# Sliding-window attention and a SoLU MLP: head pairs in one score tile, casting loads, and a list-scheduled order

## The chip, the core and the metric

The kernel runs on one core of a Trainium2 chip. TensorE (PE) multiplies matrices, VectorE (DVE) and ScalarE (ACT) do elementwise work, GpSimd (POOL) does small work and can issue transfers, SyncE (SP) issues transfers; sixteen DMA engines carry them. TensorE writes only to PSUM, 16 KB in each of 128 partitions, in eight banks of 512 fp32 columns; the other tiles lie in SBUF. The metric is the device time of one execution in microseconds (us).

## The reference

There are 4 batches of 8 heads, 768 positions and 64 dimensions per head. A query attends to the 96 latest keys (itself among them) and to the first 8 keys of the sequence, with a bias that falls with distance. The result goes through an MLP with a SoLU activation and a LayerNorm, on 3,072 tokens of 512 features with 1,024 hidden ones.

```python
scores = q @ k.T / sqrt(64)
is_global = pos_k < 8;  is_local = (0 <= rel) & (rel < 96)       # rel = pos_q - pos_k
dist = where(is_global & ~is_local, 96, abs(rel))
scores = where(is_global | is_local, scores - slope[h] * dist, -1e9)
attn = softmax(scores) @ v
x = attn.transpose(0, 2, 1, 3).reshape(3072, 512)
h = x @ w_in
solu = h * softmax(h)
ln = (solu - mean(solu)) / sqrt(var(solu) + 1e-6) * g_ln
out = ln @ w_out
```

## The kernel before

The work is written as two loops one after the other, in a framework that places semaphores and keeps each engine's instructions in program order.

First come constants: `bmask` holds, for each head, the exponential of the bias for a block of 128 keys against 256 queries, zero outside the window; `gmask` serves the global keys. The weights are loaded in fp32 by two transfers on SP (L108, L111) and cast to fp16 on VectorE (L109, L115).

The attention loop (L128) runs over batches and groups of four heads. Two heads are loaded side by side into `qq32` and `kk32` in fp32 (SP, L137 and L141), cast by ScalarE (L147, L149), transposed by TensorE in 128-column blocks into `pqQ` and `pqK` (L157, L159) and copied out by VectorE (L164, L165). v is loaded by SP (L179) and cast by POOL into `vo65`, which has a column of ones behind the 64 dimensions (L185). The global scores of four heads share the tile `psg` (L196, L201, ScalarE L207). Each head then has: six score matmuls, 128 keys against 256 queries each, into `psb` (L230); one exponential over 1,536 columns (L238); one multiplication by the mask (L249); 17 matmuls into `psav`, with the probabilities as weights and v as the moving operand, so that rows are queries and the 65th column is the divisor (L263); the reciprocal and the scaling on VectorE (L279, L285); six transposes into `pxt` (L291) and a copy into `xT` (L295), which holds the attention output with features on partitions. `psb` and `psg` share one buffer of the tag `sc`, so that a head's scores wait until the exponential of the head before has read them. `xT` holds all 3,072 tokens.

The MLP loop (L309) runs over 24 tiles of 128 tokens: eight matmuls into `ph` (L313), the exponential with its sum (L322), `solu` (L328), the mean, the sum of squares `sq` (L336), the centred `smc` (L342), eight transposes `lT` (L348), a copy `lTs` (ScalarE, L352), eight matmuls into `po` (L355) and a copy into `ouall` (L359). Only after all 24 tiles are the variances turned into `rstdall` (L361 to L378), with a square root on ScalarE that needs another function table, and each tile is then scaled and stored (L382, L386).

Of the kernel before, what the change touches and what calls it, by code (L numbers as in the profile page):

```python
# [9 lines left out]
FP32 = mybir.dt.float32  # L10
FP16 = mybir.dt.float16
I32 = mybir.dt.int32
AF = mybir.ActivationFunctionType
ALU = mybir.AluOpType

P = 128


@with_exitstack
def kernel(  # L20
# [12 lines left out]
    nc = tc.nc  # L33
# [5 lines left out]
    NSB = S // P  # L39
    NQB = 2 * P  # L40
# [3 lines left out]
    LNSC = 1024.0  # L44
# [4 lines left out]
    const = ctx.enter_context(tc.tile_pool(name="const", bufs=1))  # L49
    big = ctx.enter_context(tc.tile_pool(name="big", bufs=1))  # L50

    ident = const.tile([P, P], FP16, name="ident")
    nc.gpsimd.memset(ident, 0.0)
    nc.gpsimd.affine_select(
        out=ident, in_=ident, compare_op=ALU.not_equal, fill=1.0,
        base=0, pattern=[[-1, P]], channel_multiplier=1,
    )

    diff_i = const.tile([P, NQB], I32, name="diff_i")
    nc.gpsimd.iota(diff_i, pattern=[[1, NQB]], base=0, channel_multiplier=-1)  # L60
    diff_f = const.tile([P, NQB], FP32, name="diff_f")
    nc.vector.tensor_copy(diff_f, diff_i)
    nc.vector.tensor_scalar_max(out=diff_f, in0=diff_f, scalar1=0.0)
    bmask = const.tile([P, H, NQB], FP16, name="bmask")
    for h in range(H):
        nc.scalar.activation(out=bmask[:, h, :], in_=diff_f, func=AF.Exp,
                             scale=-slopes[h])
    bm_flat = bmask.rearrange("p h f -> p (h f)")
    nc.gpsimd.affine_select(
        out=bm_flat, in_=bm_flat, compare_op=ALU.is_ge, fill=0.0,  # L70
        base=0, pattern=[[0, H], [1, NQB]], channel_multiplier=-1,
    )
    nc.gpsimd.affine_select(
        out=bm_flat, in_=bm_flat, compare_op=ALU.is_ge, fill=0.0,
        base=NL - 1, pattern=[[0, H], [-1, NQB]], channel_multiplier=1,
    )

    gmask = const.tile([P, P], FP16, name="gmask")
    glow = const.tile([P, P], FP16, name="glow")
    nc.gpsimd.memset(glow, 1.0)  # L80
    nc.gpsimd.affine_select(
        out=glow, in_=glow, compare_op=ALU.is_gt, fill=0.0,
        base=0, pattern=[[-1, P]], channel_multiplier=1,
    )
    nc.gpsimd.memset(gmask, 1.0)
    nc.gpsimd.affine_select(
        out=gmask, in_=gmask, compare_op=ALU.is_ge, fill=0.0,
        base=-NL, pattern=[[1, P]], channel_multiplier=-1,
    )
    nc.vector.tensor_add(gmask, gmask, glow)  # L90
    gmaskq = const.tile([P, P], FP16, name="gmaskq")
    nc.gpsimd.memset(gmaskq, 1.0)
    for g in range(4):
        nc.vector.tensor_copy(gmaskq[32 * g : 32 * g + NG], gmask[0:NG])

    gbias4 = const.tile([P, 2], FP32, name="gbias4")
    for gi in range(2):
        for g in range(4):
            nc.vector.memset(
                gbias4[32 * g : 32 * (g + 1), gi : gi + 1],  # L100
                -float(NL) * slopes[4 * gi + g],
            )

    w_in_sb = const.tile([P, NCC, D_FF], FP16, name="w_in_sb")
    gw_out_sb = const.tile([P, NFC, D_MODEL], FP16, name="gw_out_sb")
    with tc.tile_pool(name="wtmp", bufs=1) as wtmp:
        w_in32 = wtmp.tile([P, NCC, D_FF], FP32, name="w_in32")
        nc.sync.dma_start(out=w_in32, in_=moe_w_in.rearrange("(j p) f -> p j f", p=P))  # L108
        nc.vector.tensor_copy(w_in_sb, w_in32)  # L109
        w_out32 = wtmp.tile([P, NFC, D_MODEL], FP32, name="w_out32")  # L110
        nc.sync.dma_start(out=w_out32, in_=moe_w_out.rearrange("(j p) c -> p j c", p=P))  # L111
        g32 = wtmp.tile([P, NFC], FP32, name="g32")
        nc.sync.dma_start(out=g32, in_=moe_g_ln.rearrange("(j p) -> p j", p=P))
        for j in range(NFC):
            nc.vector.tensor_scalar_mul(  # L115
                out=gw_out_sb[:, j, :], in0=w_out32[:, j, :],
                scalar1=g32[:, j : j + 1],
            )

    xT = big.tile([P, NCC, N_TOK], FP16, name="xT")  # L120

    with tc.tile_pool(name="apsum", bufs=1, space=bass.MemoryType.PSUM) as apsum, \
         tc.tile_pool(name="asb", bufs=3) as asb, \
         tc.tile_pool(name="ahsb", bufs=6) as ahsb, \
         tc.tile_pool(name="ajsb", bufs=4) as ajsb, \
         tc.tile_pool(name="agsb", bufs=3) as agsb:

        for b in range(B):  # L128
            for gi in range(2):
                qTs, kTs, vo65s = [], [], []  # L130
                vg65 = agsb.tile([P, 65], FP16, name="vg65")
                for pj in range(2):
                    j0 = 4 * gi + 2 * pj
                    qq32 = asb.tile([P, NSB, 2 * D], FP32, name="qq32")
                    kk32 = asb.tile([P, NSB, 2 * D], FP32, name="kk32")
                    for m in range(2):
                        nc.sync.dma_start(  # L137
                            out=qq32[:, :, m * D : m * D + D],
                            in_=q[b, j0 + m].rearrange("(a p) d -> p a d", p=P),
                        )  # L140
                        nc.sync.dma_start(  # L141
                            out=kk32[:, :, m * D : m * D + D],
                            in_=k[b, j0 + m].rearrange("(a p) d -> p a d", p=P),
                        )
                    qq16 = asb.tile([P, NSB, 2 * D], FP16, name="qq16")
                    kk16 = asb.tile([P, NSB, 2 * D], FP16, name="kk16")
                    nc.scalar.copy(out=qq16.rearrange("p a d -> p (a d)"),  # L147
                                   in_=qq32.rearrange("p a d -> p (a d)"))
                    nc.scalar.copy(out=kk16.rearrange("p a d -> p (a d)"),  # L149
                                   in_=kk32.rearrange("p a d -> p (a d)"))  # L150

                    pqQ = apsum.tile([P, NSB, P], FP16, name="pqQ",
                                     space=bass.MemoryType.PSUM, tag="pq", bufs=2)
                    pqK = apsum.tile([P, NSB, P], FP16, name="pqK",
                                     space=bass.MemoryType.PSUM, tag="pq", bufs=2)
                    for a in range(NSB):
                        nc.tensor.transpose(out=pqQ[:, a, :],  # L157
                                            in_=qq16[:, a, :], identity=ident)
                        nc.tensor.transpose(out=pqK[:, a, :],  # L159
                                            in_=kk16[:, a, :], identity=ident)  # L160
                    qTt = ajsb.tile([P, NSB + 1, P], FP16, name="qTt")
                    kTt = ajsb.tile([P, NSB, P], FP16, name="kTt")
                    nc.gpsimd.memset(qTt[:, NSB, :], 0.0)
                    nc.vector.tensor_copy(out=qTt[:, 0:NSB, :], in_=pqQ)  # L164
                    nc.vector.tensor_copy(out=kTt, in_=pqK)  # L165
                    for m in range(2):
                        qTs.append(
                            qTt[64 * m : 64 * m + D].rearrange("d a p -> d (a p)")
                        )
                        kTs.append(  # L170
                            kTt[64 * m : 64 * m + D].rearrange(
                                "d a p -> d (a p)"
                            )
                        )

                    for m in range(2):
                        g = 2 * pj + m
                        v32 = asb.tile([P, NSB, D], FP32, name="v32")
                        nc.sync.dma_start(  # L179
                            out=v32,  # L180
                            in_=v[b, j0 + m].rearrange("(a p) d -> p a d", p=P),
                        )
                        vo65 = ahsb.tile([P, NSB, 65], FP16, name="vo65")
                        nc.gpsimd.memset(vo65[:, :, D : D + 1], 1.0)
                        nc.gpsimd.tensor_copy(out=vo65[:, :, 0:D], in_=v32)  # L185
                        vo65s.append(vo65)
                        nc.vector.tensor_copy(
                            out=vg65[32 * g : 32 * g + NG], in_=vo65[0:NG, 0, :]
                        )
# [232 lines left out]
```

## Time and profile before

| quantity | value |
|---|---|
| median of 3 runs | 334.15 us (332.35 to 337.17) |
| span of the profiled execution | 335.8 us |
| busy: PE, DVE, ACT, POOL | 247.5, 191.3, 144.8, 28.9 us |
| DMA | 29.65 MB in 81,349 packets, 76,720 of them under 512 bytes |
| DMA share of 16 engines | 38.4% |
| from issue to landing, one head of q, k, v | 3.9, 4.2, 3.8 us |

The profile is of one execution. An engine is busy while an instruction of its own runs; matmuls overlap, and their ends are modelled, so that the distance from start to start tells more of TensorE's rate than the mean duration does. A group is written as line, engine, operation, output and inputs, shapes, count, then busy time and mean time of one, then the idle time just before and what ended it. The chain of waits is followed back from the last instruction to whatever released each step.

### The profile page before, as it was taken

The numbers are of one execution on the slowest core, as the hardware profiler recorded it, in microseconds if no ns is written. First come the engines' busy times: TensorE is split into PE (matmuls) and PEld (weight loads), VectorE is DVE, ScalarE is ACT, GpSimd is POOL, SyncE is SP. The second block draws the span as 40 slices with busy tenths as digits, with TensorE's granted clock in tenths as the row PEclk, the third lists the DMA queues.
The fourth block names the chain that finished last, engine by engine and source line by source line (L and its number), as shares of the span: only waits on it lengthen the run. The fifth ranks groups of instructions, "written<-read, shape, count | busy, mean of one in ns | idle before, by whom it ended". The sixth has DMA issues, their size and how long they took to land.

```text
span 335.8 us, 4686 instructions
## 1 busy us (share of the span) xinstructions
PE 247.5 (74%) x1760; PEld 140.0 (42%) x1760; DVE 191.3 (57%) x450; ACT 144.8 (43%) x179; POOL 28.9 (9%) x94
## 2 busy tenths in 40 slices
PE   0005797996969789798897887999889898895400
PEld 0002454664646466564664533444444444442100
DVE  1523364572756656364464528685965957865653
ACT  4012652536544363651634304655565656554100
POOL 7002101121101211110100000000000000000000
PEclk9999999999995755555555559999999999997755
DMA  7679966662777665368000000000000000000586
GB/s 273 227 143 217 196 125 126 127 127 47 142 143 141 142 126 107 60 133 164 2 0 0 2 0 0 2 0 2 2 0 2 0 0 2 0 0 1 197 302 250
DMA packets 81349, 29.65 MB, mean 88 GB/s; under 512 B 76720, under 2 KB 76720, under 8 KB 81328
## 3 DMA queue, kind: packets, MB, share of 16 engines
q1 hardware_dynamic: 81328, 29.37, 38.4%
q8 instruction: 13, 0.21, 0.3%
q14 instruction: 8, 0.07, 0.1%
HBM read 23.07 MB, written 6.29 MB: 87 GB/s over the span
## 4 chain that ended last, share of the span: by engine, by line
PE 49%; ACT 18%; DVE 16%; DMA 10%; issue 4%; SPq 2%; DVEq 0%; ACTq 0%
PE psb L230 13%; PE po L355 9%; PE psav L263 8%; ACT eb L238 7%; PE pxt L291 6%; DVE solu L328 6%; DMA out_dram<-osb 4%; DMA g<-in_moe_g_ln_dram 4%; ACT lTs L352 3%; PE pqK L159 3%; PE pqQ L157 3%; PE psg L196 3%; DVE sq L336 3%; ACT e L322 3%; PE ph L313 2%
## 5 line engine op out<-in xcount | busy, mean ns | idle before, releaser
L238 ACT ACTIVATE eb<-psb 128x1536 f16<-128x1536 f32 x32 | 46.4, 1451 | 52.0 <-PE psb L230 51.7
L230 PE MATMUL psb<-qTt,kTt 64*128 64x256 f16 x192 | 45.6, 395 | 18.9 <-ACT eb L238 15.0
L313 PE MATMUL ph<-w_in_sb,xT 128*128 128x512 f16 x192 | 49.9, 394 | 7.2 <-DVE solu L328 6.6
L355 PE MATMUL po<-gw_out_sb,lTs 128*128 128x512 f16 x192 | 48.4, 398 | 5.0 <-ACT lTs L352 3.8
L249 DVE TENSOR_TENSOR eb<-eb,bmask 128x1536 f16<-128x1536 f16 x32 | 30.5, 952 | 19.3 <-ACT eb L238 19.3
L230 PEld LDWEIGHTS <-kTt 64*128 64x128 f16 x192 | 22.0, 125 | 34.8 <-issue 26.5
L157 PE MATMUL pqQ<-ident,qq 128*128 128x128 f16 x96 | 14.9, 309 | 27.1 <-ACT qq L147 27.1
L355 PEld LDWEIGHTS <-lTs 128*128 128x128 f16 x192 | 17.9, 101 | 39.0 <-ACT lTs L352 20.1
L328 DVE SCALAR_TENSOR_TENSOR solu<-e,r,ph 128x1024 f16<-128x1024 f16 x24 | 30.7, 1280 | 2.7 <-DVE r L325 0.3
L322 ACT ACTIVATE e<-ph 128x1024 f16<-128x1024 f32 x24 | 24.6, 1027 | 15.7 <-PE ph L313 15.6
L359 ACT CAST ouall<-po 128x512 f16<-128x512 f32 x24 | 14.1, 586 | 36.7 <-PE po L355 36.7
L336 DVE CUSTOM_DVE_ANT_0 sq<-solu 128x1024 f16<-128x1024 f16 x24 | 29.2, 1216 | 0.0
L291 PE MATMUL pxt<-ident,onrm 128*64 128x128 f16 x192 | 26.1, 305 | 2.2 <-DVE onrm L285 2.1
L313 PEld LDWEIGHTS <-xT 128*128 128x128 f16 x192 | 18.4, 101 | 22.1 <-issue 5.5
L352 ACT COPY lTs<-lT 128x1024 f16<-128x1024 f16 x24 | 24.3, 1011 | 7.2 <-PE lT L348 7.2
L279 DVE RECIPROCAL rl<-psav 128x6 f32<-128x6 f32 x32 | 6.3, 196 | 33.5 <-PE psav L263 33.3
L263 PE MATMUL psav<-vo,eb 128*128 128x65 f16 x352 | 25.1, 243 | 0.0
L295 DVE COPY xT<-pxt 64x768 f16<-64x768 f16 x32 | 17.6, 549 | 12.7 <-PE pxt L291 12.6
L291 PEld LDWEIGHTS <-onrm 128*64 128x64 f16 x192 | 18.7, 159 | 14.2 <-DVE onrm L285 9.3
L263 PEld LDWEIGHTS <-eb 128*128 128x128 f16 x352 | 20.9, 130 | 7.8 <-issue 4.4
L147 ACT CAST qq<-qq 128x768 f16<-128x768 f32 x16 | 13.2, 824 | 22.7 <-DMA qq<-in_q_dram 22.7
L157 PEld LDWEIGHTS <-qq 128*128 128x128 f16 x96 | 9.4, 137 | 32.4 <-ACT qq L147 29.9
(63 smaller groups left out, 253.5 us busy)
## 6 DMA issues: line engine op xcount, KB each, us to landing
qq<-in_q_dram SPq DMA_DIRECT2D x32, 192.0 KB, 3.9
kk<-in_k_dram SPq DMA_DIRECT2D x32, 192.0 KB, 4.2
v<-in_v_dram SPq DMA_DIRECT2D x32, 192.0 KB, 3.8
out_dram<-osb SPq DMA_DIRECT2D x24, 256.0 KB, 2.0
w_in<-in_moe_w_in_dram SPq DMA_DIRECT2D x1, 2048.0 KB, 7.9
w_out<-in_moe_w_out_dram SPq DMA_DIRECT2D x1, 2048.0 KB, 13.9
g<-in_moe_g_ln_dram SPq DMA_DIRECT2D x1, 4.0 KB, 13.7
```

What stands on the lines that cost most here:

```text
L157: nc.tensor.transpose(out=pqQ[:, a, :], in_=qq16[:, a, :], identity=ident)
L230: nc.tensor.matmul(out=psb[:, cj, :], lhsT=kT[:, ts(cj, P)], rhs=qTp[:, ds(P * cj, NQB)], start=st, stop=not st,)
L238: nc.scalar.activation(out=eb.rearrange("p a f -> p (a f)"), in_=psb.rearrange("p a f -> p (a f)"), func=AF.Exp, scale=inv_sqrt_d,)
L249: nc.vector.tensor_tensor(out=eb.rearrange("p a f -> p (a f)"), in0=eb.rearrange("p a f -> p (a f)"), in1=bm_ap, op=ALU.mult,)
L263: nc.tensor.matmul(out=psav[:, rb, :], lhsT=lhs, rhs=rhs_ap, start=st, stop=last, tile_position=tp,)
L291: nc.tensor.transpose(out=pxt[0:D, rb, :], in_=onrm[:, rb, :], identity=ident,)
L313: nc.tensor.matmul(out=ph[:, ds(fh * 512, 512)], lhsT=xT[:, j, ts(tb, P)], rhs=w_in_sb[:, j, ds(fh * 512, 512)], start=(j == 0), stop=(j = ...
L322: nc.scalar.activation(out=e, in_=ph, func=AF.Exp, accum_out=s0)
L328: nc.vector.scalar_tensor_tensor(out=solu, in0=e, scalar=r, in1=ph, op0=ALU.mult, op1=ALU.mult, accum_out=s1,)
L336: nc.vector.tensor_tensor_reduce(out=sq, in0=solu, in1=solu, scale=1.0, scalar=0.0, op0=ALU.mult, op1=ALU.add, accum_out=s2all[:, tb : tb ...
L352: nc.scalar.copy(out=lTs, in_=lT)
L355: nc.tensor.matmul(out=po, lhsT=lTs[:, u, :], rhs=gw_out_sb[:, u, :], start=(u == 0), stop=(u == NFC - 1),)
```

## The change

The kernel is written anew around one list of steps.

*Scores.* A block is now 56 local keys; the 8 global keys stand beside them, which makes 64 rows. Two heads share the 128 rows of one score tile: matmuls of one head use rows 0 to 63 of the array, those of the other rows 64 to 127. Each block meets the 152 queries that can see it. A row of 768 queries is cut into two score groups, of 1,008 columns each, in the single PSUM tile `sc`. `mask` holds the exponential of the bias in the same layout, global keys included.

*Outputs.* v goes into `vbd`, a tile with the two heads' values in the two diagonal quarters and zeros in the others. It is the weight, the probabilities are the moving operand, and the result stands transposed, with features on partitions, as the MLP needs it; `pxt` and its copies are gone. The divisors come from matmuls with ones (`onesd`), then Ln and Exp(-x) on ScalarE (`lns`, `rr`), and a transfer on SP that spreads each pair's two rows over 128 partitions (`rb`). Sums, divisors, value matmuls and `xT` are made per half row of 384 queries.

*Loads.* All loads of q, k, v, w_in and w_out are issued by POOL and write fp16 (w_out stays fp32); the casts are gone. The global values are loaded once (`vg16`) and copied by SP into each batch's `vbd`.

*MLP.* The mean is taken out of the weights (`weight_rows`, `weight_mean`, `weight_sub`), and `uu` is e times h, divided by no sum: the LayerNorm's scale takes it in. The squares go to ScalarE. Statistics are made for three tiles at a time, by Ln and Exp(-x/2), so that there is one function table; each tile is scaled while it is copied out of PSUM and stored at once.

*Order.* `Plan` takes every step with its engine, an assumed duration, a target time, its dependencies and the buffers that it takes and frees, and places the steps in time: on each engine, of the steps that are ready, the one with the earliest target goes first. The instructions are issued in that order. Targets interleave batch b's attention with the MLP tiles of earlier rows.

```diff
+class Plan:
+    def order(self):
...
+                while heap:
+                    tgt, i = heapq.heappop(heap)
+                    s = steps[i]
+                    if s["take"] is not None and not pools[s["take"]]:
+                        kept.append((tgt, i))
+                        continue
...
+    sc_ps = [ps.tile([P, 2, 512], FP32, name="sc")]
+    ph_ps = [ps.tile([P, D_FF], FP32, name="ph")]
+    po_ps = [ps.tile([P, D_MODEL], FP32, name="po")]
+    ta_ps = [ps.tile([P, 512], FP32, name=f"ta{i}") for i in range(3)]
...
+    def load_rows(src, dst, b, p, lo, hi):
+        for h in range(2):
+            nc.gpsimd.dma_start(
+                out=dst[:, lo:hi, h, :],
+                in_=src[b, 2 * p + h].rearrange("(a p) d -> p a d", p=P)[:, lo:hi])
...
+                nc.gpsimd.dma_start(
+                    out=dst[part : part + BLK, c0 : full[-1] + 1 : 2, p, 64 * h : 64 * h + D],
+                    in_=src)
...
+    vz_st = step("POOL", 8.0, 24.0, [], lambda: nc.gpsimd.memset(vbd[1], 0.0))
...
-                    for cj in range(NSB):
-                        nc.tensor.matmul(
-                            out=psb[:, cj, :],
-                            lhsT=kT[:, ts(cj, P)],
-                            rhs=qTp[:, ds(P * cj, NQB)],
...
+                        for c, q0, w, par, col in PIECES[gi] + PADS[gi]:
+                            for h in range(2):
+                                o = 64 * (h ^ par)
+                                nc.tensor.matmul(
+                                    out=sc[o : o + 64, par, col : col + w],
+                                    lhsT=kk[64 * h : 64 * h + D, c, :],
+                                    rhs=qq[64 * h : 64 * h + D, q0 : q0 + w],
+                                    start=True, stop=True, tile_position=(64 * h, o),
+                                )
...
+                        nc.tensor.matmul(
+                            out=sp[32 * p : 32 * p + 32, lo : lo + w], lhsT=onesd[:, par, :],
+                            rhs=eb[e_st[p, gi][0]["slot"]][:, par, col : col + w],
...
+                            tile_position=(0, 32 * p), skip_group_check=True,
...
+                    nc.sync.dma_start(
+                        out=rb[ri_["slot"]],
+                        in_=bass.AP(tensor=a.tensor, offset=a.offset,
+                                    ap=[a.ap[0], [0, 4], [1, HS]]))
...
+                        nc.tensor.matmul(
+                            out=o[:, lo : lo + w], lhsT=vbd[vi["slot"]][:, c, p, :],
+                            rhs=eb[e_st[p, gi][0]["slot"]][:, par, col : col + w],
...
-            nc.vector.scalar_tensor_tensor(
-                out=solu, in0=e, scalar=r, in1=ph,
-                op0=ALU.mult, op1=ALU.mult, accum_out=s1,
-            )
+        u["fn"] = lambda u=u, ex=ex, gidx=gidx, gcol=gcol: nc.vector.scalar_tensor_tensor(
+            out=uu[u["slot"]], in0=ef[ex["slot"]], scalar=USC, in1=ph_ps[0],
+            op0=ALU.mult, op1=ALU.mult, accum_out=s1[gidx][:, gcol : gcol + 1])
...
+                ou["fn"] = lambda ou=ou, gidx=gidx, x=x: nc.scalar.activation(
+                    out=osb[ou["slot"]], in_=po_ps[0], func=AF.Copy,
+                    scale=rstd[gidx][:, x % 3 : x % 3 + 1])
...
+    for s in plan.order():
+        if s["fn"] is not None:
+            s["fn"]()
```

## The prediction

> **What bounds the kernel now.** I read four views, in this order. The first is a table of stages: the span cut at the points where the work changes, with the busy time of each engine (instructions in brackets), the granted clock, the DMA share and GB/s.
>
> ```profile
> 0.00:32.00 32.00, 4.11 (x28) 2.36 (x28) 9.97 (x30) 7.16 (x13) 8.28 (x27) 1.00 0.86 215
> 32.00:197.00 165.00, 138.89 (x1156) 90.16 (x1156) 90.43 (x194) 73.79 (x68) 20.65 (x67) 0.72 0.52 99
> 197.00:312.00 115.00, 101.63 (x570) 46.73 (x571) 79.49 (x204) 63.25 (x97) 0.00 (x0) 0.96 0.00 1
> 312.00:335.80 23.80, 2.92 (x8) 0.76 (x6) 11.45 (x24) 0.59 (x1) 0.00 (x0) 0.57 0.71 264
> ```
>
> There are four stages one after the other: 32 us of loading weights, 165 us of attention, 115 us of MLP, 24 us in which the output is only scaled and stored. The DMA engines are empty for 115 us, TensorE nearly so for the 56 us of the outer two.
>
> The second view is the page's chain of work that ended last.
>
> ```profile
> PE 49%; ACT 18%; DVE 16%; DMA 10%; issue 4%; SPq 2%; DVEq 0%; ACTq 0%
> PE psb L230 13%; PE po L355 9%; PE psav L263 8%; ACT eb L238 7%; PE pxt L291 6%; DVE solu L328 6%; DMA out_dram<-osb 4%; DMA g<-in_moe_g_ln_dram 4%; ACT lTs L352 3%; PE pqK L159 3%; PE pqQ L157 3%; PE psg L196 3%; DVE sq L336 3%; ACT e L322 3%; PE ph L313 2%
> ```
>
> TensorE carries half of it, handing over to ScalarE and back (psb to eb): in attention nothing else is ready while one hand-over runs.
>
> The third view is the timeline of TensorE (start, duration, line, count).
>
> ```profile
> 91.27 0.61 PE L196 MATMUL psg<-qTt,kTt 64*32 64x512 f16 x2
> 93.55 0.52 PE L263 MATMUL psav<-vo,eb 128*128 128x65 f16 x11
> 94.00 0.35 PE L263 MATMUL psav<-vg,eg 8*128 8x65 f16 x6
> 95.16 0.39 PE L196 MATMUL psg<-qTt,kTt 64*32 64x512 f16 x2 [0.65 <-DVE kTt L165]
> 95.38 0.28 PE L201 MATMUL psg<-qTt,kTt 64*32 64x256 f16 x2
> 99.01 0.89 PE L230 MATMUL psb<-qTt,kTt 64*128 64x256 f16 x6 [1.54 <-ACT eb L238]
> ...
> 103.16 1.46 PE L230 MATMUL psb<-qTt,kTt 64*128 64x256 f16 x6
> ```
>
> Two things show. Six psb matmuls take 0.89 us at 99 us but 1.46 at 103: the clock changes between full and half. The six take 1.44 to 1.46 nearly everywhere in attention, so attention runs at half clock almost throughout, though the page's PEclk row shows 9 in its first twelve slices; durations decide. And the two psg matmuls of 512 columns, one on each 64-row half of the array, start 0.22 us before the next pair (95.16 to 95.38), which is the time of one: halves run side by side. In the MLP eight 512-column matmuls take 1.73 us (0.216 each), and 3.61 just after 197 us, before the clock rises.
>
> The fourth view is the groups, for prices:
>
> ```profile
> L238 ACT ACTIVATE eb<-psb 128x1536 f16<-128x1536 f32 x32 | 46.4, 1451 | 52.0 <-PE psb L230 51.7
> L249 DVE TENSOR_TENSOR eb<-eb,bmask 128x1536 f16<-128x1536 f16 x32 | 30.5, 952 | 19.3 <-ACT eb L238 19.3
> L328 DVE SCALAR_TENSOR_TENSOR solu<-e,r,ph 128x1024 f16<-128x1024 f16 x24 | 30.7, 1280 | 2.7 <-DVE r L325 0.3
> L322 ACT ACTIVATE e<-ph 128x1024 f16<-128x1024 f32 x24 | 24.6, 1027 | 15.7 <-PE ph L313 15.6
> ```
>
> **The change, priced.** The profiled execution has a span of 335.8 us; the median of the runs is 334.15 (332.35 to 337.17), 0.5% less. I work in spans and do not correct. Under 2% is about what a measurement of this kernel cannot tell from no change.
>
> *Merging the stages.* MLP tiles are woven into attention, so the four lines of the first table no longer add. The new time is a start until the first MLP tile, then the busiest resource, then a tail. Each resource needs its sum.
>
> *TensorE at full clock.* MLP: 384 matmuls of 512 columns x 0.216 = 83. Transposes of uu: 192 x 0.056 (eight take 0.45 in the MLP) = 11. Transposes of q and k: 204 x 0.056 = 11. Scores: 544 small matmuls, 64x152 at most, at the 41 ns from start to start of the eleven psav above (0.45 us) = 22. Sums: 256 x 0.041 = 10.5. Value matmuls: 16 head pairs x 2,000 columns at 512 per 0.216 us = 13.5. Weight means: eight fp32 matmuls of 512 columns; the trace has none in fp32, so 0.216 each (2) or four times that (7); I take 7, the safe end. Sum 158, against 247.5 busy now. At half clock: MLP 384 x 0.45 = 173, transposes 396 x 0.105 (six pqQ in 0.62 at 110 us) = 42, small ones 800 x 0.067 (eleven psav in 0.74 at 100 us) = 54, values 27, means 14: 310.
>
> *ScalarE.* Now 144.8. The q and k casts (26.5), eg (7.2) and lTs (24.3) go; the exponential shrinks from 32 x 1.45 to 32 x about 1.02 (1,008 columns, near the 1,027 ns of L322); the squares come in (24 x 1.23 with the accumulator read, the price of e). Adding 16 divisor steps at about 0.45, 24 scaled copies at 0.59 and mask building, 16 x 0.6: 2 x 29.5 + 32.6 + 7 + 14 + 10 = 123. Not the bound.
>
> *VectorE.* Now 191. 24 x 1.36 (uu), 24 x 0.7 (uT; from 549 ns for 768 columns, L295), 32 x 0.65 (mask, from L249), 32 x 0.55 (xT, like L285), 16 x 1.3 (kT, qT), about 20 for masks, statistics and weights: 129. Not the bound. sq, smc, reciprocals, rl and the last 24 scalings go.
>
> *DMA.* The q, k and v loads keep 73,728 packets of 256 bytes. In a steady attention stretch (120 to 150 us) the share is 0.61 at 119 GB/s: 293 us of engine time for 13,950 packets, 21 ns each. 73,728 x 21 / 16 = 97. Weights: both land by 15.7 us, 12. Output 17 (0.71 x 23.8 us). The broadcasts rr to rb move as many bytes as the output in rows a little shorter: 17 to 20. Sum 145, below TensorE, if a casting packet costs what a plain one does. The trace has no casting transfer. Between half (it writes half the bytes) and twice the price I take the same, the row it is nearest to.
>
> *POOL.* All 172 loads are now issued there; beside them it has 8 weight scalings (about 0.77 each, from the cast L185), a 7,168-column memset (about 5, from 205 ns for 128 columns and 124 for 6) and constants. A blocked load (its k16 or vbd buffer not yet free) holds every later load. No load is issued from POOL in the trace; the SP rows give 0.37 to 1.14 us per issue as the lower bound, and 3.9 us to landing as the upper. At 0.4 to 0.8 the queue is busy 69 to 138 us, hidden.
>
> *The start.* In POOL's order the first q/k parts (7,168 packets, 9.4 us), w_in and w_out (12), parts of the next (2,048 packets, 2.7) and v's first half (3,136 packets, 4.1) go before the first value matmul. From 2 us, with 2 us to land: 32; four xT products make it 35. Mask building on VectorE (24 operations of about 0.25) and the vbd memset (3,584 columns at POOL's 0.66 ns, 2.4) hide under these loads.
>
> *Added waits.* The value matmul waits for sums, Ln, Exp and a broadcast on SP (about 0.4 + 0.45 + 0.45 + 2 us landing, by the output rows' 2.0). Behind it on TensorE stands whatever the list put there; the planner spaces these 5 us apart, so it costs little unless TensorE runs ahead of plan. Scores have one PSUM tile: each score group waits for the exponential before (1.02 us), during which MLP matmuls are queued.
>
> *The tail.* The 24 us of scaling and stores shrink to the last tile's chain: squares 1.2, statistics 0.7, Ln and Exp 0.4, copy 0.6, store 2.0, some overlapped: 6.
>
> *The sum.* 35 + remaining TensorE work + 6. Of 158, 5 are done before the first tile: 153. How well does a stream fill? The MLP now takes 13.38 us for 3 tiles (po starting at 238.44, 251.82, 265.21), 4.46 a tile, with 3.9 of work: a factor of 1.14. Two interleaved streams should lie between 1.00 and that; with the half clock still to return at times I take 1.10: 169. 35 + 169 + 6 = **210 us**. With factors 1.00 and 1.25 this case runs from 190 to 232.
>
> The Trainium skill, "TensorE: Matmul & The Clock Gate", Part 1, says the clock halves after an idle window of about 3.4 us and rises after a busy one. The trace disagrees with the first half: attention has no idle stretch that long after 34 us and yet is at half clock. By the rule the new kernel never goes cold and the factor is 1.00, 194 us; by the rows it may.
>
> The same skill, "SBUF — State Buffer", section "SBUF: two separate sides", warns that a VectorE copy from SBUF to SBUF starves descriptor writing for POOL-issued loads. No run here shows it. In the steady part VectorE reads PSUM or two tensors, so it would concern the masks at the start only, some 6 us more.
>
> **The rivals.**
>
> *The clock stays down half the time.* For: attention work now holds it down at 84% busy TensorE. Against: the MLP's 512-column matmuls raised it within 4 us of 197, and they are over half of the new work. Halfway between 153 and 300 is 227: 35 + 227 + 6 = 268. All at half clock: 341, no change.
>
> *Transfers set the pace.* At twice the packet price q, k and v need 194 instead of 97: 242 in all, plus the last batch's six tiles (27): 270. For: cast, short packets. Against: the share now is 0.52.
>
> *POOL's issuing becomes the bound, and the kernel is slower.* One queue now writes every load's packets. It decides from the point where an issue takes (341 - 35) / 172 = 1.8 us; at 2.2 us, over half of the 3.9 us to landing, 172 x 2.2 + 20 = 398. For: 768 packets per issue, by a processor that also computes. Against: SP's 0.4 to 1.1 us for the same shape.
>
> *It fits exactly.* Casting packets at half price take 8 off the start (27), the factor is 1.00: 27 + 153 + 6 = 186, and 181 with the weight means at 2.
>
> **How the numbers follow.** Forecast 0.62; half clock 0.15; transfers 0.12; POOL 0.08; exact fit 0.03. I predict 210. The range 180 to 285 takes in the forecast, the transfers and most of the half-clock case; it leaves out POOL and the clock's far end, which is 0.14 or so. Faster by over 2%: all but POOL and the far end of the clock, 0.88; within 2%: 0.03; slower: 0.09.
>
> **What would show it.** Right: TensorE over 80% busy between 35 and 200 us, eight 512-column matmuls at 1.73 us in most places, first ph near 35, DMA share near 0.7, no storing stage. Half clock: eight take 3.4. Transfers: TensorE's waits end at q16, k16 or vbd. POOL: the DMA share falls below 0.5 while TensorE waits for loads. My sum is wrong if score pairs do not run side by side (then 544 x 63 ns, 12 us more) or if small matmuls wait for their weights.

## The result, and the profile after

The changed kernel takes 274.23 us (median of 4 runs, 271.51 to 276.63) beside 335.66 us for the kernel before: a ratio of 0.816 (0.808 to 0.825). The profiled execution, with a span of 274.9 us, is the slowest of the four (276.63 us at a granted clock of 0.881; the others have 0.887 to 0.898). I had predicted 210 and a range of 180 to 285: the sign is right, but the gain is half of the one forecast. Where did 65 us go?

First the same cut by stages. The columns are stretch, length, busy time of PE, PEld, DVE, ACT and POOL, then clock, DMA share and GB/s. A DMA share over 1 means that the times of several packets on one engine overlap. I cut where the MLP tiles change their rhythm.

```profile
40.00:52.00 12.00, 8.10 (x69) 5.30 (x69) 3.96 (x13) 1.74 (x3) 10.90 (x16) 1.00 1.01 109
52.00:76.00 24.00, 0.43 (x18) 0.34 (x17) 1.38 (x3) 2.32 (x4) 24.00 (x27) 0.58 0.63 42
76.00:121.00 45.00, 31.54 (x319) 16.97 (x323) 19.91 (x47) 13.95 (x21) 38.51 (x51) 0.77 1.25 97
121.00:255.00 134.00, 114.70 (x1296) 67.61 (x1296) 74.46 (x155) 81.23 (x142) 39.64 (x53) 0.95 0.72 105
255.00:275.00 20.00, 9.77 (x37) 3.46 (x34) 3.08 (x8) 4.73 (x9) 0.00 (x0) 0.73 0.10 39
```

From 52 to 76 us TensorE works 0.43 us, VectorE and ScalarE 1.4 and 2.3; POOL is busy for every one of the 24 us. From 121 to 255 TensorE is busy 86% of the time. The loss is ahead of 121 us.

The timeline of POOL in that gap (start, duration, line, count) shows what it does.

```profile
51.80 10.82 POOL L355 DMA_DIRECT2D vbd<-in_v_dram  x16
62.61 1.31 POOL L366 DMA_DIRECT2D vbd<-in_v_dram  x2
63.91 6.09 POOL L410 MEMSET vbd<- 128x7168 f16 x1
69.92 1.70 POOL L342 DMA_DIRECT2D k<-in_k_dram  x2
```

And the timeline of TensorE:

```profile
52.32 0.43 PE L523 MATMUL sc<-qT,kT 64*64 64x104 f16 x18 [0.55 <-ACT eb L531]
76.19 0.91 PE L472 MATMUL ta<-ident,k 128*128 128x128 f16 x7 [23.43 <-DMA k<-in_k_dram]
76.89 3.38 PE L645 MATMUL ph<-w_in_sb,xT 128*128 128x512 f16 x8
...
90.76 2.08 PE L311 MATMUL po<-w_out,ones 128*128 128x512 f32 x2 [9.71 <-POOL w_out L306]
```

TensorE waits 23.43 us for a load of k that was issued only at 69.92, behind 18 issues for v and a memset. The second MLP tile follows directly behind that wait. The first tile's half row had given the input of three tiles, so this one was ready; it stood behind the transposes in TensorE's order. Its eight matmuls take 3.38 us, half clock, after the long wait (the granted clock is 0.50 from 64 to 76 us). A second long wait follows: at 90.76 TensorE has stood 9.71 us for the scaled rows of w_out. POOL scales them only from 89.96 on, after 26 more issues behind the memset.

The page's chain and three of its groups (busy time, mean ns | idle before):

```profile
PE 38%; POOL 21%; DMA 17%; ACT 8%; issue 7%; DVE 7%; SPq 1%; ACTq 0%; DVEq 0%; POOLq 0%
...
q0 software_dynamic: 82112, 12.64, 60.3%
...
L699 PE MATMUL po<-gw_out_sb,uT 128*128 128x512 f16 x192 | 50.2, 409 | 10.5 <-ACT osb L704 10.1
L355 POOL DMA_DIRECT2D vbd<-in_v_dram x80 | 56.3, 726 | 0.6 <-DMA q<-in_q_dram 0.5
L342 POOL DMA_DIRECT2D k<-in_k_dram x40 | 32.6, 827 | 10.1 <-PE ta L472 9.5
```

POOL, absent from the chain before, has 21% of it. One issue costs it 0.73 to 0.83 us. The loads that it issues (queue q0) fill 60.3% of the sixteen engines' span: their 256-byte packets that are cast on the way have a median and a mean of 32 ns in the transfer records, where I had taken 21, a mean of plain ones.

For the experiments I use one count, read off the timeline of TensorE: when the first and the fourth of the 24 MLP tiles start (the first `ph` matmul of each), how long the twenty from the fourth on take, and what is left from the start of the last tile to the end. My sum in these terms: 35 + 3 x 7.04 = 56 us, 20 x 7.04 = 141, and 7 + 6 = 13.

| kernel | time, us | ratio to before (95%) | 1st tile at | 4th tile at | us per tile | rest |
|---|---|---|---|---|---|---|
| forecast | 210 | | 35 | 56 | 7.04 | 13 |
| changed kernel | 274.23 | 0.816 (0.808 to 0.825) | 47.5 | 121.3 | 6.69 | 19.8 |
| e1 buffers in turn | 262.84 | 0.790 (0.784 to 0.797) | 47.3 | 120.5 | 6.00 | 19.9 |
| e2 prices told to the plan | 290.13 | 0.863 (0.851 to 0.875) | 41.5 | 92.7 | 8.85 | 19.7 |
| e3 e1 and e2 | 281.94 | 0.840 (0.830 to 0.849) | 41.8 | 94.2 | 8.24 | 20.0 |
| e6p plain q and k, cast by POOL | 262.91 | 0.787 (0.780 to 0.795) | 65.0 | 97.3 | 7.10 | 19.7 |
| e5 memset, scalings off POOL | 257.72 | 0.773 (0.762 to 0.784) | 82.1 | 115.2 | 6.06 | 19.8 |
| e8 e1, a third of q and k | 258.84 | 0.779 (0.763 to 0.794) | 46.6 | 117.2 | 5.97 | 20.0 |
| e9 e1, each load issued twice | 288.19 | 0.862 (0.842 to 0.881) | 60.0 | 142.7 | 6.19 | 20.0 |
| e6 e1, two `po` tiles | 251.89 | 0.757 (0.744 to 0.769) | 47.3 | 118.8 | 5.76 | 14.8 |
| e10 e6 and e5 | 244.27 | 0.724 (0.720 to 0.728) | 81.0 | 112.2 | 5.80 | 15.1 |
| e12 e10, v behind k and q | 231.35 | 0.693 (0.687 to 0.699) | 68.5 | 98.8 | 5.81 | 14.0 |
| e11 e10, plain q and k, cast by ACT and DVE | 226.29 | 0.671 (0.668 to 0.674) | 55.1 | 90.3 | 6.02 | 14.0 |

For the changed kernel: the fourth tile at 121.32, the last at 255.11, so (255.11 - 121.32) / 20 = 6.69, and 274.9 - 255.1 = 19.8. Against the forecast the fourth tile is 65 us late, the twenty tiles are 7 us quicker, the rest takes 7 us longer. Of the 65, 12.5 lie ahead of the first tile (47.5 for 35); the other 53 lie between the first and the fourth (73.8 us, where I had 21). What fails is the stretch up to the fourth tile, below called the start.

### The profile page after: what moved, and what is told of

Same layout as the page of the kernel before. It is cut to its first block, busy times and chain, and to the rows that moved or that the text cites. A ratio compares the mean times of both kernels' runs of the same rounds, so it can differ in the third digit from the quotient of the medians.

```text
span 274.9 us, 4775 instructions
## 1 busy us (share of the span) xinstructions
PE 172.6 (63%) x1852; PEld 99.0 (36%) x1852; DVE 120.5 (44%) x274; ACT 119.8 (44%) x201; POOL 143.9 (52%) x220
## 3 DMA queue, kind: packets, MB, share of 16 engines
q0 software_dynamic: 82112, 12.64, 60.3%
q1 hardware_dynamic: 10128, 13.51, 19.3%
## 4 chain that ended last, share of the span: by engine, by line
PE 38%; POOL 21%; DMA 17%; ACT 8%; issue 7%; DVE 7%; SPq 1%; ACTq 0%; DVEq 0%; POOLq 0%
PE po L699 13%; PE ph L645 11%; POOL vbd L355 8%; DMA out_dram<-osb 5%; DMA rb<-rr 4%; POOL k L342 4%; POOL q L342 4%; PE po L311 3%; DMA w_in_sb<-in_moe_w_in_dram 3%; PE ta L664 3%; ACT ef L650 3%; ACT osb L704 3%; PE sc L523 2%; DMA q<-in_q_dram 2%; POOL vbd L410 2%
## 5 line engine op out<-in xcount | busy, mean ns | idle before, releaser
L699 PE MATMUL po<-gw_out_sb,uT 128*128 128x512 f16 x192 | 50.2, 409 | 10.5 <-ACT osb L704 10.1
L355 POOL DMA_DIRECT2D vbd<-in_v_dram x80 | 56.3, 726 | 0.6 <-DMA q<-in_q_dram 0.5
L650 ACT ACTIVATE ef<-ph 128x1024 f16<-128x1024 f32 x24 | 24.5, 1021 | 71.1 <-PE ph L645 70.9
L531 ACT ACTIVATE eb<-sc 128x1008 f16<-128x1008 f32 x32 | 32.1, 1005 | 26.5 <-PE sc L523 26.4
L653 DVE SCALAR_TENSOR_TENSOR uu<-ef,ph 128x1024 f16<-128x1024 f16 x24 | 29.2, 1217 | 20.5 <-ACT ef L650 20.2
L342 POOL DMA_DIRECT2D k<-in_k_dram x40 | 32.6, 827 | 10.1 <-PE ta L472 9.5
L342 POOL DMA_DIRECT2D q<-in_q_dram x40 | 32.1, 818 | 5.8 <-PE ta L472 5.1
L535 DVE TENSOR_TENSOR eb<-eb,mask 128x1008 f16<-128x1008 f16 x32 | 21.7, 680 | 24.9 <-ACT eb L531 24.9
L606 PE MATMUL ta<-eb,vbd 128*128 128x152 f16 (+4 forms) x256 | 19.3, 228 | 17.7 <-DMA vbd<-vg 13.8
L657 ACT ACTIVATE sq<-uu 128x1024 f16<-128x1024 f16 x24 | 25.3, 1055 | 8.9 <-DVE uu L653 8.9
L704 ACT ACTIVATE osb<-po,rstd 128x512 f32<-128x512 f32 x24 | 16.5, 686 | 22.2 <-DMA out_dram<-osb 10.1
L523 PE MATMUL sc<-qT,kT 64*64 64x152 f16 (+5 forms) x544 | 14.8, 233 | 5.8 <-ACT eb L531 3.6
```

The costliest lines, as they stand in the source:

```text
L342: nc.gpsimd.dma_start(out=dst[:, lo:hi, h, :], in_=src[b, 2 * p + h].rearrange("(a p) d -> p a d", p=P)[:, lo:hi])
L355: nc.gpsimd.dma_start(out=dst[part : part + BLK, c0 : full[-1] + 1 : 2, p, 64 * h : 64 * h + D], in_=src)
L523: nc.tensor.matmul(out=sc[o : o + 64, par, col : col + w], lhsT=kk[64 * h : 64 * h + D, c, :], rhs=qq[64 * h : 64 * h + D, q0 : q0 + w], s ...
L531: ex["fn"] = (lambda ex=ex: nc.scalar.activation(out=eb[ex["slot"]], in_=sc_ps[0][:, :, 0:GC], func=AF.Exp, scale=inv_sqrt_d))
L535: mk["fn"] = (lambda ex=ex, p=p, gi=gi: nc.vector.tensor_tensor(out=eb[ex["slot"]].rearrange("p n c -> p (n c)"), in0=eb[ex["slot"]].rearr ...
L606: nc.tensor.matmul(out=o[:, lo : lo + w], lhsT=vbd[vi["slot"]][:, c, p, :], rhs=eb[e_st[p, gi][0]["slot"]][:, par, col : col + w], start=( ...
```

## The experiments

Theory A says that transfers set the pace: the casting packets fill the engines until 182 us. (The engines are indeed busy until then, but the last casting packet ends at 172 us; behind it come broadcasts.) It was my second rival, and the trace has its announced sign: TensorE's waits end at loads. B, in the first four runs, lays it to what the plan chose, order and buffers. C was formed after them: POOL's one in-order queue of issues holds the start back, and afterwards the single PSUM tiles of the MLP set the pace.

One caution holds for what follows: `Plan` places all steps anew whenever a duration or a dependency changes. In e1, e8 and e9 TensorE, VectorE and ScalarE run the same instructions in the same order as in the changed kernel; in the other runs their order differs too, so that an edit there changes more than its own lines.

**Buffers in turn (e1).** The planner hands out the free buffer with the lowest number, and so the one used last.

```diff
                     pools[name].append(slot)
-                    pools[name].sort()
```

> Edit: a buffer that comes free goes to the end of its pool's list, so that buffers are taken in turn and not the lowest number first; nothing else. Theory A (the casting loads, at 32 ns a packet, keep the sixteen DMA engines full until 182 us and set the pace to there; 12 of the 24 tiles are behind them): the load stream ends no earlier than 175 us, and only the waits of osb on its store (10 us) and of rr on its broadcast (9 us) go: 262 to 274 us. Theory B (the list's order rests on wrong prices and on buffers used again too soon, so that in-order queues block): POOL's waits for k16 and q16 (15 us) go, the last 12 tiles close up from 6.7 to about 5.5 us each: 245 to 258 us.

262.84 us, in A's range and not in B's: POOL's waits for free `k16` and `q16`, which B had going, only shrink from 14.6 to 11.3 us. The start is nearly unchanged (120.5), the pace goes from 6.69 to 6.00. The list of waits of the changed kernel (total, times, longest) has the cause:

```profile
ACT osb L704 <- DMA out_dram<-osb: 10.1, 5, 3.6
PE po L699 <- ACT osb L704: 10.1, 9, 2.6
ACT rr L583 <- DMA rb<-rr: 9.2, 2, 5.1
```

`osb` has three buffers, but a tile's copy waited for the store of the tile before, and `po` for that copy. With buffers in turn the first and the third wait are gone from the list.

**True prices for the planner (e2, e3).** The plan assumed 0.25 us per issue and 1.73 us per load.

```diff
-        iss = step("POOL", 0.25 * n_iss, target, deps, None, lat=0.0, **kw)
+        iss = step("POOL", 0.8 * n_iss, target, deps, None, lat=0.0, **kw)
...
-                us = 1.73 / NA
+                us = 3.1 / NA
```

(and 3.5 for 1.9, 0.8 for 0.3 in the v loads; e3 has e1's edit too.)

> Edit: the planner is told what the profile measured for loads (0.8 us of POOL an issue in place of 0.25; 3.1 us of DMA for a pair's q or k in place of 1.73, 3.5 in place of 1.9 for v); the same instructions in another order. Theory A: transfers stay as they are, the end moves only as far as MLP tiles move in front of the last loads: 262 to 278 us, loads end at 175 us or later. Theory B: the 23 us in which TensorE stands before the second batch's k with a tile ready behind it go, and more: 235 to 255 us.

> Both edits, buffers in turn and measured prices for the planner. Theory A: 255 to 272 us. Theory B: the gains of both add, 225 to 245 us.

Both theories miss: 290.13 and 281.94 us. The fourth tile comes 28.6 us earlier (92.7), but then twenty tiles take 8.85 us each. Between the tile at 107.98 and the next at 139.61 of e2 no MLP tile starts; TensorE is busy for 20.1 of the 32 us from 108 to 140, over half of it with attention, and waits for ScalarE and VectorE with little to put between. Truer prices alone made a worse mixture. The targets had stayed as they were, which may be why; I did not follow this further.

**Plain transfers (e6p).** SP loads q and k in fp32 into four staging tiles; POOL casts.

```diff
-            nc.gpsimd.dma_start(
+            nc.sync.dma_start(
...
+                    dma["fn"] = lambda raw=raw, ld=ld, k_or_q=k_or_q, lo=lo, hi=hi: nc.gpsimd.tensor_copy(
```

> Edit: q and k are loaded by SP without a cast, fp32 into four staging tiles, and POOL casts them (about 1.1 us a tile); v stays as it is. 96 fewer issues on POOL (some 75 us of its queue) for 35 us of casts, and 49,152 packets at 18 to 21 ns in place of 32. Theory A: 49,152 x 12 ns / 16 = 37 us of DMA time go, loads end near 145 us and the run at 235 to 250 us. Theory B (order, not transfers): loads end earlier, but TensorE's order is the same and its waits move to other lines: 255 to 275 us.

262.91 us, in B's range and not in A's. (POOL issues 80 loads fewer here, not 96.) The plain 256-byte packets cost 18 ns (median), and POOL's queue ends at 153 us instead of 169.5; yet the first tile starts at 65.0, later than before (47.5), because POOL's casts stand behind its v issues: TensorE waits 40.1 us in all for `k` from POOL. The fourth tile comes 24 us earlier all the same, but the twenty behind it slow to 7.10 us each. Cheaper packets did not bring the time that A had. As issues and packets changed together, this run does not tell which of the two moved the fourth tile.

**Work off POOL (e5).**

```diff
-    vz_st = step("POOL", 8.0, 24.0, [], lambda: nc.gpsimd.memset(vbd[1], 0.0))
+    vz_st = step("DVE", 6.0, 14.0, [masks_st], lambda: nc.vector.memset(vbd[1], 0.0))
...
-        nc.gpsimd.tensor_scalar(out=w_out32[:, j, :], in0=w_out32[:, j, :],
-                                scalar1=g32[:, j : j + 1], scalar2=0.0,
-                                op0=ALU.mult, op1=ALU.add)
+        nc.scalar.activation(out=w_out32[:, j, :], in_=w_out32[:, j, :], func=AF.Copy,
+                             scale=g32[:, j : j + 1])
```

> The changed kernel with two pieces of POOL's work moved off POOL: the 6.09 us memset of the second vbd buffer goes to VectorE near the start, the eight weight scalings (756 ns each, 6.0 us) to ScalarE. The loads, their order on POOL and their packets stay. Theory C (POOL's one in-order queue holds the first tiles back; each microsecond taken out of it comes off the start): 258 to 266 us, the batch-1 k wait of 23 us shorter by 6 or more, last load issue near 157 instead of 168 us. Theory A (the 32 ns casting packets fill the DMA engines until 182 us and set the pace): 271 to 276 us, the last load still lands near 180 us.

257.72 us, and the last issue ends before 160 us, nearly as C had it. But the table splits the gain otherwise than C did: 6 us in the start, and the larger part in the pace, 6.69 to 6.06. The changed order also eases the wait of `osb` for its stores, from 10.1 to 3.3 us. And the longest wait for k grew, to 28.5 us, where C had it shrink: with the memset gone, 18 more v issues stand ahead of that k, which is issued at 77.30 instead of 69.92. TensorE's wait of 9.71 us for the scaled rows, on the other hand, is gone. So of 12 us taken off POOL, half is seen at the start.

**A second po tile (e6).** On e1, one of the three `ta` tiles becomes a second `po`.

```diff
-    po_ps = [ps.tile([P, D_MODEL], FP32, name="po")]
-    ta_ps = [ps.tile([P, 512], FP32, name=f"ta{i}") for i in range(3)]
+    po_ps = [ps.tile([P, D_MODEL], FP32, name=f"po{i}") for i in range(2)]
+    ta_ps = [ps.tile([P, 512], FP32, name=f"ta{i}") for i in range(2)]
```

> The kernel with buffers taken in turn (262.84 us), and po given a second PSUM tile, taken from the transposes (two instead of three). Theory C (after the start the pace of 6.1 to 6.3 us a tile is set by the chain through the single ph and po tiles): 246 to 256 us, the wait of the second MLP matmul for the output's eviction nearly gone, pace 5.5 us a tile or less. Theory A (transfers set the pace): 260 to 266 us, the same waits on data remain.

251.89 us: 5 us in the pace (5.76; the 5.5 expected were not reached), 5 in the rest, where one group of `po` matmuls instead of two is left to do after the last statistics. Its waits list has

```profile
PE po L698 <- ACT osb L703: 4.4, 2, 2.6
```

where e1 had 8.5. The transfers are the same, so this speaks against A.

**Bytes without issues, issues without bytes (e8, e9).** These two part A from C. Both stand on e1 and keep its order on TensorE, VectorE and ScalarE.

```diff
     def load_rows(src, dst, b, p, lo, hi):
+        hi = hi if b == 0 else lo + 2
```

> The kernel with buffers taken in turn (262.84 us), but every q and k load of batches 1 to 3 brings only two of the six row blocks; the rest of the tile keeps older rows. Number and order of all instructions stay, POOL's issues too; 24576 casting packets of 32 ns are gone, 49 us of the 16 engines' time. Theory C (POOL's issuing and the single PSUM tiles): 256 to 264 us. Theory A (transfers set the pace): 214 to 238 us.

```diff
+        m = (lo + hi) // 2
         for h in range(2):
-            nc.gpsimd.dma_start(
-                out=dst[:, lo:hi, h, :],
+            for l, u in ((lo, m), (m, hi)):
+                nc.gpsimd.dma_start(
+                    out=dst[:, l:u, h, :],
```

> The kernel with buffers taken in turn (262.84 us), but each q and k load is issued as two halves: 80 more POOL issues, the same packets. Theory C (POOL's issuing sets when the tiles start): 80 times 0.6 to 0.8 us, 48 to 64 us more on POOL, most of it seen: 290 to 325 us, last load issue at 210 to 230 us. Theory A (transfers set the pace, POOL hidden): 260 to 268 us.

e8 takes 258.84, e9 288.19 us. Two lines of e1's page, the queue of POOL's loads and the k loads, and the same two of e8's:

```profile
q0 software_dynamic: 82112, 12.64, 63.5%
...
L341 POOL DMA_DIRECT2D k<-in_k_dram x40 | 32.8, 831 | 8.0 <-PE ta L471 7.3
```

```profile
q0 software_dynamic: 57536, 9.50, 44.7%
...
L342 POOL DMA_DIRECT2D k<-in_k_dram x40 | 29.9, 759 | 10.4 <-PE ta L472 9.0
```

A third of the casting packets is gone, and with it 3.3 us of the start; the pace stays (6.00 and 5.97). A had 214 to 238 us. (The intervals of e1 and e8 overlap, so that even this gain is not certain.) An issue of a third of the packets is little cheaper for POOL: over the k loads of batches 1 to 3, the only ones that were cut, the mean goes from 869 to 749 ns. In e9 the bytes are the same and the fourth tile comes 22.2 us later:

```profile
L343 POOL DMA_DIRECT2D k<-in_k_dram x80 | 57.4, 732 | 0.5 <-DMA vbd<-in_v_dram 0.5
```

Issues of half the size cost nearly as much as whole ones (732 ns for 831). Even the first tile comes 12.7 us later, at 60.0. A has fallen for what comes behind the first tile; since e8 leaves batch 0's loads whole, it says nothing of what comes before. C's size was a little high: 288 where it had at least 290. POOL is busy 192.6 us instead of 144.1, and of these 48 us 25 are seen.

**Together (e10).** e6 with e5's two edits.

> Buffers in turn, two po tiles (251.89 us), and with them the memset and the weight scalings off POOL. If what those two saved alone (17 us: 274.2 to 257.7) lies in the start and what the second po tile saved (11 us) in the pace, they add up: 233 to 242 us. Theory A (transfers set the pace): no less than 248 us, since the packets are the same.

244.27 us, a little over C's range. The start gains 6.6 us, much as in e5 alone; the pace stays at 5.80, where e5 alone had gained: in e6 `osb` no longer waited for its stores. The timeline of POOL in e10, and below it TensorE's:

```profile
63.54 11.51 POOL L353 DMA_DIRECT2D vbd<-in_v_dram  x16
75.04 1.28 POOL L364 DMA_DIRECT2D vbd<-in_v_dram  x2
76.32 1.69 POOL L340 DMA_DIRECT2D k<-in_k_dram  x2
...
80.31 0.91 PE L470 MATMUL ta<-ident,k 128*128 128x128 f16 x7 [27.48 <-DMA k<-in_k_dram]
```

TensorE waits 27.48 us for that k, with 18 more v issues ahead of it than in e6, as in e5. While k had no free buffer in the plan, v had one, and went first.

**Place in the queue (e12).** One edit to e10; no instruction more or less.

```diff
-        vi = step("POOL", 0.0, tv, [zero_st] + ([vz_st] if b == 1 else []), None, take="vbd",
+        vi = step("POOL", 0.0, tv, [zero_st] + ([vz_st] if b == 1 else []) + ([bufs[1, "q16"]] if b else []), None, take="vbd",
```

> The kernel with buffers in turn, two po tiles and memset and scalings off POOL (244.27 us), with one thing changed: the v loads of a batch may be issued only after the k and q loads of that batch's first two head pairs. In its trace 18 v issues (12.8 us, from 63.5 to 76.3) stood on POOL ahead of the first k load of batch 1, for which TensorE waited 27.5 us. The number of issues, of packets and of instructions stays. Theory C (it is the place in POOL's order): the k load is issued near 63 us, the wait falls by 10 to 13 us, 230 to 238 us. Theory A, or a theory that the sum of POOL's work counts and not its order: 241 to 247 us.

231.35 us, 12.9 less for 12.8 us of issues moved. The k load is issued at 63.77 instead of 76.32, and TensorE's wait for it falls by 9.8 us, a little under the 10 that C had at least. The intervals of e10 and e12 are far apart. The order on the other engines changed with the plan too, so the run is not as clean as its one edit. TensorE's timeline in e12:

```profile
67.74 0.91 PE L470 MATMUL ta<-ident,k 128*128 128x128 f16 x7 [17.67 <-DMA k<-in_k_dram]
68.45 3.62 PE L643 MATMUL ph<-w_in_sb,xT 128*128 128x512 f16 x8
```

The fourth tile comes 13.4 us earlier, the pace is the same (5.80, 5.81). Later on TensorE is nearly full:

```profile
99.00:215.00 116.00, 108.64 (x1291) 64.80 (x1289) 73.99 (x155) 80.35 (x142) 47.36 (x63) 1.00 1.05 131
```

**Fewer issues on POOL (e11).** e10, with e6p's plain loads, but cast by ScalarE (k) and VectorE (q).

```diff
-                    dma["fn"] = lambda raw=raw, ld=ld, k_or_q=k_or_q, lo=lo, hi=hi: nc.gpsimd.tensor_copy(
+                    dma["fn"] = lambda raw=raw, ld=ld, nm=nm, k_or_q=k_or_q, lo=lo, hi=hi: (
+                        nc.scalar.activation if nm == "k" else nc.vector.tensor_copy)(
```

> The kernel before this one in the same call (buffers in turn, two po tiles, memset and scalings off POOL), but q and k are loaded uncast by SP into four staging tiles and cast by ScalarE (k) and VectorE (q); POOL issues 80 loads fewer, about 65 us of its queue, and 73984 casting packets fall to about 30000. Theory C: POOL's queue ends near 75 us, the tiles flow from 65 to 80 us on, and 24 tiles at 5.6 us with the tail end the run at 210 to 228 us. Against it: the casts (56 of some 0.8 us) come into the MLP's chain on the two engines and the pace falls back to 6.5 us a tile: 232 to 245 us.

226.29 us, the fastest kernel of the study, at the upper end of C's range: 0.671 (0.668 to 0.674) of the kernel before. The fourth tile comes at 90.3 instead of 112.2; the pace is a little slower (6.02), perhaps for the casts. POOL is busy 68.9 us instead of 131.5, though not done by 75 us, since later v loads wait for their buffer. The packets of q and k changed here along with the issues; that the gain comes from the issues rests on e8 and e9.

**The start of e11 put in order (e13).** `vg` is zeroed earlier, w_in loaded behind `vg`, w_out by SP.

```diff
-    zero_st = step("DVE", 3.0, 9.0, [masks_st], constants_zero)
+    zero_st = step("DVE", 5.0, 3.0, [masks_st], constants_zero)
...
-        out=w_in_sb, in_=moe_w_in.rearrange("(j p) f -> p j f", p=P)), 1, 5.1, 7.0, [])
-    w_out_iss, w_out_st = load(lambda i: nc.gpsimd.dma_start(
+        out=w_in_sb, in_=moe_w_in.rearrange("(j p) f -> p j f", p=P)), 1, 5.1, 7.0, [vg_iss])
+    w_out_iss, w_out_st = load_sp(lambda i: nc.sync.dma_start(
```

> The fastest kernel so far (226.29 us: q and k uncast by SP) with its start put in order: the zeroing of vg on VectorE ahead of the first casts (POOL's loads of v waited 11.7 us for it), w_in loaded after vg, w_out loaded by SP after w_in. If the start still costs there (TensorE is busy 10 of the first 40 us), 215 to 222 us; if the casts and the 5.6 us a tile set the time, 224 to 229 us.

242.37 us, and no answer. Its waits list shows a new one:

```profile
DVE vbd L409 <- DMA vbd<-in_v_dram: 32.3, 1, 32.3
```

In this plan the memset of the second `vbd` buffer fell behind the first loads of v into it: VectorE stands 32.3 us for them, and those values are set to zero, so that part of the attention output is left out. How much of e11's start can still be had stays open.

## Why the prediction was right in sign and wrong in size

*The step that failed* is "At 0.4 to 0.8 the queue is busy 69 to 138 us, hidden", and with it the start of 35 and the even 7.04 us a tile behind it. The price was inside its bounds: 0.77 us on average, 128 us for 172 issues. But I compared 138 us with the whole span, and most of the queue's work comes ahead of the stage in which TensorE could hide it.

For the start I counted the transfers' engine time (28 us) and not the issues ahead of the first value matmul. Those are 42 (16 of the first q/k parts, 2 weights, 6 of the next, 2 `vg`, 16 v): 30.5 us on POOL's timeline, with 7.4 us of its own waits and 5.4 of constants, so that the last v is issued at 43.3; the first tile came at 47.5. Of batch 1, k comes behind 70 issues and the memset, and TensorE stands 23.43 us for it; the scaled rows come behind 26 more, and TensorE stands 9.71 us for them. e9 shows the effect of more issues with all else kept, e12 that of the place in the queue, e11 that of fewer issues (with cheaper packets).

How far does it reach? The fourth tile goes from 121.3 to 98.8 us through e5's edits and the order, and to 90.3 with 80 issues taken off POOL. From there to 56 some 34 us remain which no run takes apart. e11's trace says where they lie: its first tile comes at 55.1, 20 us after the forecast, and from there to the fourth TensorE is busy 26.6 of 35.2 us, so that most of this stretch is work, part of which I had spread over the later tiles: the twenty that follow take 20 us less than forecast. Ahead of the first tile transfers may have a part, too: in the changed kernel POOL's 7.4 us of waits end at landings, and the DMA share is 1.01 to 1.05 from 20 to 47.5 us.

*The added wait.* I wrote that it "costs little unless TensorE runs ahead of plan". It was not TensorE that ran ahead: the loads fell behind the plan, which had 0.25 us per issue. What I did not name is what then stands behind a blocked step in TensorE's order, the MLP tile at 76.89.

*TensorE's work, 158.* It is busy 172.6 us here, 161.4 to 163.4 in e6, e10, e11 and e12: nearly right for a kernel that flows. The sign that I had set, over 80% busy between 35 and 200 us, failed: 112.3 of 165 us, 68%. The factor of 1.10 for the stream: 134 / 114.7 = 1.17 from 121 to 255 us, 116 / 108.6 = 1.07 in e12. I had laid it to the interleaving and the clock; the order of `osb` and `rr` buffers (e1, with the same instructions) made most of the difference, and the second `po` (e6, in another order) some more. By my own sum the factor 1.00 gives 194, not the 190 that I wrote.

*ScalarE 123, VectorE 129:* 119.8 and 120.5. Score pairs do run side by side (18 in 0.43 us).

*DMA 145.* The casting packet costs 32 ns, 1.5 times the 21 I took, inside the bounds. In all, the packets of queues q0 and q1 (60.3 and 19.3% of the span) add up to 219 us, far over 145 and over the forecast itself; as they overlap, that is no lower bound. Taking a third of the casting packets away moved the start by 3.3 us (e8), in which POOL's cheaper issues have a part, and not the pace.

*The tail, 6* after the last tile's matmuls, or 13 from its start: 19.8, of which the single `po` made 5 (e6).

*The rivals.* The transfers' case gave 270 us, near the time measured, and its sign was seen: TensorE's waits end at k and vbd. But a load that comes late because it was issued late gives the same sign, and e8 decides against the transfers behind the first tile. So the time of 270 was near by luck, and the measured time lies in my range only because the range took in that case and the half clock. POOL's case had the right place and the wrong price: below 1.8 us an issue it was not to matter. It announced a DMA share below 0.5 while TensorE waits for loads; from 64 to 70 us it was 0.12, over the whole gap from 52 to 76 us 0.63. *The clock* did not stay down: of the 48 groups of eight 512-column matmuls seven took 3.17 to 3.57 us, among them those behind the waits of 23.43 us (at 76.89) and of 2.58 us (`po` at 262.73), one took 2.71, and the other forty 1.89 to 1.97.

The Trainium skill, "Perfetto Trace Analysis", section "What 'DMA-bound' means", names this case: the issuing engine's track is solid with DMA work, and that time is the writing of descriptors, not the moving of data. POOL is solid from 52 to 76 us, 6 of these 24 us with the memset. It goes on that large descriptors are what matters there. No run here changes the size of the q, k and v packets, but their number per issue counted for little: a third of the packets made an issue 14% cheaper (869 to 749 ns), while twice the issues with the same packets took 25 us more (e9). Here it was the number of issues that counted.

## What to carry to other kernels

Price an issuing engine in the stage where its work comes first, one issue after the other, and look at what stands behind each load on its queue; that it is hidden over the whole span says nothing of the start. Where a wait ends at a load, take bytes away with the issues kept, and then add issues with the bytes kept: the wait itself does not tell which it is. Hand buffers out in turn; the lowest free number is the one that was just used.

## What the runs showed of the hardware

A 256-byte packet that is cast to 128 bytes takes 32 ns, a plain one loaded by SP 18 (e6p). An issue on POOL costs 0.7 to 0.87 us almost whatever its size: in the changed kernel two issues of 384 packets take 1.51 us, two of 768 take 1.70. An issue on SP takes about 0.5 us in e11 (two in 1.09) while its queue isn't held up; at other places there two take up to 8.63. In e12 the records give a clock of 1.00 throughout, yet eight `ph` matmuls took 3.62 us after the wait of 17.67 us, and 1.9 in the other 23 tiles: the durations show a half clock that the records do not.
